# Normalised x of later batches computed by tokens and transposed by DMA, with its steps, banks and loads rearranged

## The chip, the cores and the metric

The kernel runs on one core of one Trainium2 chip. The metric is the device time of one execution in microseconds (us). A profiled execution shows a span about 2 us shorter than the device time (319.4 us for 321.2 before), so spans are compared with spans and times with times.

## The reference

Linear attention, an RMS norm per head, and a bilinear feed-forward:

```
kv  = einsum('bhsd,bhse->bhde', k, v)          # 8 batches, 8 heads, 576 tokens, head size 64
x   = einsum('bhsd,bhde->bhse', q, kv)
x   = x / sqrt(mean(x*x, over the 64) + 1e-6) * g_norm
x   = x.transpose(0, 2, 1, 3).reshape(4608, 512)
out = ((x @ w_a) * (x @ w_b)) @ w_out          # 512 -> 1536 -> 512
```

## The kernel before

x is kept transposed in SBUF (feature on the partition, token along the row), because the kernel's feed-forward takes it so as `rhs`. The profile shows a matmul as two records: a load of the one operand, its weights (`lhsT`, 128x128 in 98 ns in the feed-forward), and a pass over the columns of the other (`rhs`, 512 columns from one start to the next in 0.216 us). Results go to PSUM, used here as eight banks of 128 x 512 numbers (`P[:, 0]` to `P[:, 7]`). The kernel writes a bank anew only when its last reader is done; in the changed kernel TensorE waits for that twice, 0.58 us each. The feed-forward goes over nine strips of 512 tokens. While TensorE works on strip s, the x of batch s+1 is put between its matmuls, in "slots": slot(n) comes after unit n of the strip, slot(n - 0.5) in the middle of unit n. A unit is one block of 128 features of the hidden layer: four matmuls with w_a (part a), four with w_b (part b), all 512 columns wide. Units 12 to 15 of the count are the four output groups. With FC = 12, a strip has 12 x 8 + 4 x 12 = 144 matmuls of 512 columns.

```
def x(self, p, i0):                    # a pair of heads: 2 matmuls of 288 columns
    for h in range(2):
        nc.tensor.matmul(P[:, i0 + h, 0:HF], lhsT=kvb[self.b % 2][:, p, :],
                         rhs=self.qT[:, p, h * HF : (h + 1) * HF], start=True, stop=True)

def psq(self, p, i0):                  # square, ScalarE
    nc.scalar.activation(sq[p % 3], P[:, i0 : i0 + 2, 0:HF], AF.Square)

def pss(self, p, i0, hs=(0, 1)):       # mean over the head's 64 partitions: 2 more matmuls
    for h in hs:
        nc.tensor.matmul(P[:, i0 + h, 0:HF], lhsT=ones, rhs=sq[p % 3][:, h, :], start=True, stop=True)
    nc.scalar.activation(rs[p % 3][...], P[...], AF.Abs_reciprocal_sqrt, bias=eps_t)

def pst(self, p, x0, hs=(0, 1)):       # x * g * rs, written straight into xt
    for h in hs:
        nc.vector.scalar_tensor_tensor(out=xt[p][:, t0 : t0 + HF], in0=P[:, x0 + h, 0:HF],
                                       scalar=g_col, in1=rs[p % 3][:, h, :], ...)

# ... cut ...
def ffn_ab(s, fc, between=None):       # a unit: PSUM banks in turn out of 0, 1, 2
    i = n_ab[0]; n_ab[0] += 2
    u = Unit(s, fc, i % 3, (i + 1) % 3)
    u.part_a()                         # 4 matmuls, then ScalarE casts the bank to SBUF
    if between: between()              # slot(n - 0.5)
    u.part_b()                         # 4 matmuls, then VectorE multiplies the two

def slot(A, s, n):
    kb = P[:, 7, 0 : NP * D]...
    if s < 3: k0, xs, ss = 6, (7, 9.5, 12, 13.5), (8, 10.5, 12.5, 14)
    else:     k0, xs, ss = 2, (4, 7, 10, 12), (5, 8, 11, 13)
    if n == k0: ...  # kv of the batch: 40 small matmuls
    if n in xs: ...  # x, psq
    if n in ss: ...  # pss, pst
```

The q of batches 2 to 7 is cast to bf16 in DRAM by GpSimd's DMAs (`load_late`, with k and v of the batch) and transposed from there by a DMA that SyncE issues (`transpose_q`). In `load_late`, a tiny GpSimd copy reads the transposed q of the batch before, and so holds the loads back until that transpose has landed (the first one waits 15.02 us for it, until 62.92, and the loads follow from 63.76). SyncE also issues the stores, and in the trace its issues follow the order of the program: strip 0's stores from 46.54 us, the q transpose behind them from 53.37.

## Time and profile before

| | before |
|---|---|
| device time, median | 321.61 us (3 runs, 321.01 to 321.7) |
| span of the profiled run | 319.4 us |
| TensorE busy | 312.0 us, 98% |
| VectorE, ScalarE, GpSimd busy | 39%, 39%, 22% |

The page's table of engines (PE is TensorE's matmuls, PEld its weight loads, DVE VectorE, ACT ScalarE, POOL GpSimd; SP, further down, is SyncE):

```profile
PE 312.0 (98%) x1848; PEld 150.2 (47%) x1883; DVE 124.6 (39%) x218; ACT 125.3 (39%) x217; POOL 70.2 (22%) x94
```

Busy time alone would not prove that TensorE is the limit. The windows view of strips 1, 2 and 3 (columns: window, its length, then busy us and count of each engine, clock, DMA share, GB/s) comes nearer: 33.7 of 33.9 us.

```profile
50.37:84.27 33.90, 33.69 (x199) 16.30 (x201) 14.33 (x25) 14.79 (x25) 6.57 (x7) 1.00 1.11 151
84.27:118.16 33.89, 33.68 (x197) 16.25 (x200) 13.35 (x22) 14.29 (x24) 12.56 (x14) 1.00 1.07 122
118.16:152.06 33.90, 33.74 (x198) 16.28 (x200) 13.45 (x22) 14.39 (x24) 7.17 (x8) 1.00 1.27 151
```

The chain of waits in strip 5 shows what the strip is made of (columns: start, length, what; L255 and L309 are the feed-forward, L158 is kv, L235 is x, L209 the mean):

```profile
191.30 0.75 PE P L158 x40
...
195.61 0.24 PE P L235 x2
195.86 1.73 PE P L255 x8
197.59 0.25 PE P L209 x2
...
214.84 5.18 PE P L309 x24
220.02 3.24 PE P L255 x15
```

24 matmuls of 512 columns take 5.18 us, 0.216 each; 144 of them take 31.1. Strip 7, which has no next batch to compute, bears this out: it takes 31.08 us (253.75 to 284.83). Four pairs for x and four for the mean, at 0.24 to 0.25 us, take about 1.95. kv takes 0.75, and about 0.1 more passes before it. TensorE's timeline shows this in strip 1 (start, length, and so on; from start to start a part of four matmuls takes 0.86 us, the lengths given are longer and overlap; the `x3` is a part with one record missing):

```profile
61.59 1.03 PE L255 MATMUL P<-xt,wb_t 128*128 128x512 bf16 x4
62.55 0.82 PE L158 MATMUL P<-vtl,ktl 128*64 128x64 bf16 x40
63.30 1.04 PE L255 MATMUL P<-xt,wa_t 128*128 128x512 bf16 x3
```

The sum is the strip, 33.9 us. So TensorE waits for no other engine in the middle strips, and work taken off it shortens them; a better order of the same matmuls promises little there.

### The profile page before, as it was taken

The numbers are of one execution on the slowest core, as the hardware profiler recorded it, in microseconds if no ns is written. First come the engines' busy times: TensorE is split into PE (matmuls) and PEld (weight loads), VectorE is DVE, ScalarE is ACT, GpSimd is POOL, SyncE is SP. The second block draws the span as 40 slices with busy tenths as digits, with TensorE's granted clock in tenths as the row PEclk, the third lists the DMA queues.
The fourth block names the chain that finished last, engine by engine and source line by source line (L and its number), as shares of the span: only waits on it lengthen the run. The fifth ranks groups of instructions, "written<-read, shape, count | busy, mean of one in ns | idle before, by whom it ended". The sixth has DMA issues, their size and how long they took to land.

```text
span 319.4 us, 4695 instructions
## 1 busy us (share of the span) xinstructions
PE 312.0 (98%) x1848; PEld 150.2 (47%) x1883; DVE 124.6 (39%) x218; ACT 125.3 (39%) x217; POOL 70.2 (22%) x94
## 2 busy tenths in 40 slices
PE   8899999999999999999999999999999999999995
PEld 3444454444445444444444444444544444444443
DVE  5543344444244333452245324532364243313421
ACT  3733165354335443542445225542454323123310
POOL 8944990070043080350070000000000000000000
PEclk9999999999999999999999999999999999999999
DMA  8999999999379999899499150003000200020002
GB/s 182 197 196 199 201 182 230 141 95 161 99 92 159 135 123 211 81 138 173 119 94 129 66 139 2 0 35 100 0 2 14 90 30 0 34 84 18 0 33 99
DMA packets 79308, 32.60 MB, mean 102 GB/s; under 512 B 49974, under 2 KB 74806, under 8 KB 79286
## 3 DMA queue, kind: packets, MB, share of 16 engines
q0 software_dynamic: 59120, 18.44, 53.0%
q1 hardware_dynamic: 19810, 13.44, 17.1%
q10 hardware_dynamic: 356, 0.43, 0.4%
q8 instruction: 14, 0.23, 0.3%
q14 instruction: 8, 0.07, 0.1%
HBM read 37.75 MB, written 12.98 MB: 159 GB/s over the span
## 4 chain that ended last, share of the span: by engine, by line
PE 93%; POOL 3%; DMA 2%; issue 1%; ACT 0%; POOLq 0%
PE P L255 58%; PE P L309 29%; PE P L209 2%; PE P L235 2%; DMA wb_t<-in_moe_w_b_dram 2%; PE P L158 2%; POOL vt L106 1%; POOL qt L106 1%; POOL kt L106 1%; PE P L182 0%; POOL wa_t L367 0%; POOL wb_t L367 0%; ACT o_end L540 0%; POOL ident masks.py:199 0%; POOL ident masks.py:197 0%
## 5 line engine op out<-in xcount | busy, mean ns | idle before, releaser
L273 DVE TENSOR_TENSOR ab<-P,asb 128x512 bf16<-128x512 f32 x108 | 74.5, 691 | 124.0 <-PE P L255 120.7
L255 PE MATMUL P<-xt,wa_t 128*128 128x512 bf16 x422 | 111.2, 379 | 0.9 <-issue 0.2
L255 PE MATMUL P<-xt,wb_t 128*128 128x512 bf16 x421 | 110.1, 379 | 0.3
L309 PE MATMUL P<-wo_t,ab 128*128 128x512 bf16 (+1 forms) x431 | 97.5, 373 | 0.7
L269 ACT CAST asb<-P 128x512 bf16<-128x512 f32 x108 | 63.0, 585 | 85.3 <-PE P L255 83.8
L255 PEld LDWEIGHTS <-wb_t 128*128 128x128 bf16 x432 | 42.3, 98 | 50.6 <-DMA wb_t<-in_moe_w_b_dram 0.5
L309 PEld LDWEIGHTS <-ab 128*128 128x128 bf16 x444 | 43.1, 98 | 45.4
L255 PEld LDWEIGHTS <-wa_t 128*128 128x128 bf16 x432 | 41.7, 98 | 45.1 <-issue 0.5
L223 DVE SCALAR_TENSOR_TENSOR xt<-P,g_col,rs 128x288 bf16<-128x288 f32 x64 | 30.1, 513 | 29.6 <-ACT rs L213 29.6
L205 ACT ACTIVATE sq<-P 128x576 bf16<-128x576 f32 x31 | 20.2, 650 | 25.1 <-PE P L235 23.2
L213 ACT ACTIVATE rs<-P,eps_t 128x576 f32<-128x576 f32 (+1 forms) x33 | 23.9, 727 | 14.9 <-PE P L209 14.6
L322 ACT COPY osb<-P 128x512 f32<-128x512 f32 x17 | 10.0, 586 | 46.0 <-PE P L309 43.6
L324 DVE COPY osb<-P 128x512 f32<-128x512 f32 x18 | 12.4, 691 | 26.9 <-PE P L309 26.8
L129 POOL DMA_DIRECT2D qs<-in_q_dram x12 | 19.6, 1636 | 2.2 <-issue 2.1
L126 POOL COPY gate<-qT 1x1 bf16<-1x1 bf16 x5 | 0.9, 176 | 83.2 <-DMA qT<-qs 83.2
L209 PE MATMUL P<-sq,ones 128*128 128x288 bf16 x64 | 13.2, 286 | 0.5 <-ACT sq L205 0.4
L235 PE MATMUL P<-qT,kvb 128*128 128x288 bf16 x56 | 11.4, 286 | 0.0
L169 ACT CAST kvb<-P 64x256 bf16<-64x256 f32 (+1 forms) x20 | 6.0, 301 | 11.1 <-PE P L158 11.0
L209 PEld LDWEIGHTS <-ones 128*128 128x128 bf16 x64 | 6.2, 98 | 7.5 <-issue 0.4
L235 PEld LDWEIGHTS <-kvb 128*128 128x128 bf16 x56 | 5.5, 98 | 6.0
L121 POOL DMA_DIRECT2D wo_t<-in_moe_w_out_dram x12 | 6.4, 530 | 6.7 <-DMA wb_t<-in_moe_w_b_dram 3.3
L337 PE MATMUL P<-zeros 128*128 128x512 bf16 x16 | 6.2, 532 | 1.2 <-DVE eps_t L352 1.2
(55 smaller groups left out, 82.6 us busy)
## 6 DMA issues: line engine op xcount, KB each, us to landing
out_dram<-osb SPq DMA_DIRECT2D x23, 256.0 KB, 2.0
qs<-in_q_dram POOLq DMA_DIRECT2D x12, 288.0 KB, 6.6
ktl<-in_k_dram POOLq DMA_DIRECT2D x6, 512.0 KB, 8.7
vtl<-in_v_dram POOLq DMA_DIRECT2D x6, 512.0 KB, 10.7
out_dram<-osb SPq DMA_DIRECT2D x13, 128.0 KB, 2.4
wo_t<-in_moe_w_out_dram POOLq DMA_DIRECT2D x12, 128.0 KB, 6.0
wa_t<-in_moe_w_a_dram POOLq DMA_DIRECT2D x5, 256.0 KB, 9.2
wb_t<-in_moe_w_b_dram POOLq DMA_DIRECT2D x5, 256.0 KB, 9.8
```

Of the source, the lines that this page charges most:

```text
L129: nc.gpsimd.dma_start(out=d[:, hs, :], in_=q[b, hs].rearrange("h t d -> t h d"))
L205: nc.scalar.activation(sq[p % 3], P[:, i0 : i0 + 2, 0:HF], AF.Square)
L209: nc.tensor.matmul(P[:, i0 + h, 0:HF], lhsT=ones, rhs=sq[p % 3][:, h, :], start=True, stop=True)
L213: nc.scalar.activation(rs[p % 3][:, h0:h1, :], P[:, i0 + h0 : i0 + h1, 0:HF], AF.Abs_reciprocal_sqrt, bias=eps_t,)
L223: nc.vector.scalar_tensor_tensor(out=xt[p][:, t0 : t0 + HF], in0=P[:, x0 + h, 0:HF], scalar=g_col, in1=rs[p % 3][:, h, :], op0=ALU.mult, o ...
L235: nc.tensor.matmul(P[:, i0 + h, 0:HF], lhsT=kvb[self.b % 2][:, p, :], rhs=self.qT[:, p, h * HF : (h + 1) * HF], start=True, stop=True,)
L255: nc.tensor.matmul(self.a if w is wa_t else self.b, lhsT=w[:, kc, self.fc * 128 : (self.fc + 1) * 128], rhs=xt[kc][:, t0 : t0 + STRIP], st ...
L269: nc.scalar.copy(self.t, self.a)
L273: nc.vector.tensor_mul(abt[self.s % 2][self.fc], self.b, self.t)
L309: nc.tensor.matmul(P[:, i, e0:e1], lhsT=abt[s % 2][fc][:, g * 128 : (g + 1) * 128], rhs=wo_t[:, fc, e0:e1], start=(fc == 0), stop=(fc == F ...
L322: nc.scalar.copy(t, P[:, i, :])
L324: nc.vector.tensor_copy(t, P[:, i, :])
```

## The change

The intent: for batches 2 to 7, compute x with tokens on the partitions instead. Then the mean over a head's 64 numbers runs along the row, and VectorE does it; the eight matmuls with `ones` go. The price is that x comes out the wrong way round for the feed-forward, so a transposing DMA puts it into `xt`. The 576 tokens of a batch are five chunks, 4 of 128 tokens and one of 64, each in one bank. Four matmuls of 128 columns make a chunk, with q as the weights.

```diff
+        def tx(self, c, i):                       # slot x
+            t0 = c * 128
+            n = min(128, S - t0)                  # 64 for the last chunk
+            for p in range(NP):
+                nc.tensor.matmul(P[0:n, i, p * 128 : (p + 1) * 128],
+                    lhsT=self.qT[:, p, t0 : t0 + n], rhs=kvb[self.b % 2][:, p, :], start=True, stop=True)
+            nc.scalar.activation(sqt[c % 3][0:n], P[0:n, i, :]..., AF.Square)
+        def tss(self, c):                         # slot x + 0.5
+            nc.vector.reduce_sum(sst[c % 3][0:n], sqt[c % 3][0:n], axis=mybir.AxisListType.X)
+        def trs(self, c):                         # slot x + 1
+            nc.scalar.activation(rst[c % 3][0:n], sst[c % 3][0:n], AF.Abs_reciprocal_sqrt, ...)
+            nc.gpsimd.tensor_mul(sqt[c % 3][0:n], rst[c % 3][0:n]..., g_all[0:n]...)
+        def txt(self, c, i):                      # slot x + 2.5
+            nc.vector.tensor_mul(t[0:n], P[0:n, i, :]..., sqt[c % 3][0:n])
+            nc.sync.dma_start_transpose(xt[:, :, t0 : t0 + n], t[0:n]...)
 ...
+    AB = (4, 1, 2, 0)                             # banks of the units, in turn; were 0, 1, 2
 ...
+    nc.sync.dma_start(out=g_all, in_=g_norm.partition_broadcast(128))
+    transpose_q(2)
     ffn_o(0, 0, X[0])                             # strip 0's output groups and stores
 ...
-    transpose_q(2)
 ...
-        if s < 3:
-            k0, xs, ss = 6, (7, 9.5, 12, 13.5), (8, 10.5, 12.5, 14)
-        else:
-            k0, xs, ss = 2, (4, 7, 10, 12), (5, 8, 11, 13)
+        k0, xs = (5, (6.5, 7.5, 8.5, 9.5, 10.5)) if s == 1 else (2, (3.5, 5, 6, 7.5, 8.5))
 ...
+        for c, x in enumerate(xs):
+            i = 5 + c % 3                         # the chunk's bank
+            if n == x:         A.tx(c, i)
+            elif n == x + 0.5: A.tss(c)
+            elif n == x + 1:   A.trs(c)
+            elif n == x + 2.5: A.txt(c, i)
 ...
+            if s == 1 and n == 3:
+                load_late(3)
+            if b + 1 < B and n == (12 if s == 1 else 8):
+                transpose_q(b + 1)
+            if b + 2 < B and n == 13:
+                load_late(b + 2)
```

(Cut: buffers, the counting of the banks, and the old lines of the loads and transposes. The four `xt` tiles become one; the buffers of the start-up are used again for x by tokens.)

More of the change, by code (lines that the diff above doesn't have):

```diff
@@ L70 @@
     kvb = [sb([128, NP, 128], BF16, f"kvb{i}") for i in range(2)]
-    xt = [sb([128, n_tok], BF16, f"xt{i}") for i in range(KC)]
+    xt = sb([128, KC, n_tok], BF16, "xt")
     abt = [[sb([128, STRIP], BF16, f"ab{i}_{f}") for f in range(FC)] for i in range(2)]
@@ L75 @@
     rs = [sb([128, 2, HF], FP32, f"rs{i}") for i in range(3)]
+    k_x = sb([128, 2 * EC * D], FP32, "k_x")
+    k32 = k_x[0:EP].rearrange("p (h c d) -> p h c d", h=2, c=EC)
+    sqt = [sb([128, H, D], FP32, f"sqt{i}") for i in range(2)]
+    sqt.append(k_x[:, 0 : H * D].rearrange("p (h d) -> p h d", h=H))
+    sst = [sb([128, H], FP32, f"sst{i}") for i in range(3)]
+    rst = [sb([128, H], FP32, f"rst{i}") for i in range(3)]
+    g_all = sb([128, D], FP32, "g_all")
     o_sb = [sb([128, d_model], FP32, f"osb{i}") for i in range(4)]
@@ L83 @@
     warm = sb([128, 1], FP32, "warm")
-    k32 = sb([EP, 2, EC, D], FP32, "k32")
-    v32 = sb([EP, 2, EC, D], FP32, "v32")
-    q32 = sb([EP, 2, EC, D], FP32, "q32")
+    qv = [sb([128, 2 * EC * D], FP32, f"qv{i}") for i in range(2)]
+    q32, v32 = (t[0:EP].rearrange("p (h c d) -> p h c d", h=2, c=EC) for t in qv)
+    x_tok = [t.bitcast(BF16).rearrange("p (c h d) -> p c h d", c=3, h=H) for t in qv]
     qc = sb([EP, EC, 2 * D], BF16, "qc")
@@ L223, in pst @@
                 nc.vector.scalar_tensor_tensor(
-                    out=xt[p][:, t0 : t0 + HF],
+                    out=xt[:, p, t0 : t0 + HF],
                     in0=P[:, x0 + h, 0:HF],
@@ L241, in x @@
                 )
+        def tx(self, c, i):
+            t0 = c * 128
+            n = min(128, S - t0)
+            for p in range(NP):
+                nc.tensor.matmul(
+                    P[0:n, i, p * 128 : (p + 1) * 128],
+                    lhsT=self.qT[:, p, t0 : t0 + n],
+                    rhs=kvb[self.b % 2][:, p, :],
+                    start=True,
+                    stop=True,
+                )
+            nc.scalar.activation(
+                sqt[c % 3][0:n], P[0:n, i, :].rearrange("t (h d) -> t h d", h=H), AF.Square
+            )
+        def tss(self, c):
+            n = min(128, S - c * 128)
+            nc.vector.reduce_sum(sst[c % 3][0:n], sqt[c % 3][0:n], axis=mybir.AxisListType.X)
+        def trs(self, c):
+            n = min(128, S - c * 128)
+            nc.scalar.activation(
+                rst[c % 3][0:n],
+                sst[c % 3][0:n],
+                AF.Abs_reciprocal_sqrt,
+                bias=eps_t[0:n],
+                scale=1.0 / D,
+            )
+            nc.gpsimd.tensor_mul(
+                sqt[c % 3][0:n],
+                rst[c % 3][0:n].unsqueeze(2).to_broadcast([n, H, D]),
+                g_all[0:n].unsqueeze(1).to_broadcast([n, H, D]),
+            )
+        def txt(self, c, i):
+            t0 = c * 128
+            n = min(128, S - t0)
+            t = x_tok[c // 3][:, c % 3]
+            nc.vector.tensor_mul(
+                t[0:n], P[0:n, i, :].rearrange("t (h d) -> t h d", h=H), sqt[c % 3][0:n]
+            )
+            t0 += self.b * S
+            nc.sync.dma_start_transpose(
+                xt[:, :, t0 : t0 + n], t[0:n].rearrange("t h d -> t (h d)")
+            )
     class Unit:
@@ L257, in mm @@
                     lhsT=w[:, kc, self.fc * 128 : (self.fc + 1) * 128],
-                    rhs=xt[kc][:, t0 : t0 + STRIP],
+                    rhs=xt[:, kc, t0 : t0 + STRIP],
                     start=(kc == KORD[0]),
@@ L277, in rest, with ab_bank @@
             self.part_b(kcs)
+    AB = (4, 1, 2, 0)
     n_ab = [0]
+    def ab_bank():
+        n_ab[0] += 1
+        return AB[(n_ab[0] - 1) % len(AB)]
     def ffn_ab(s, fc, between=None):
-        i = n_ab[0]
-        n_ab[0] += 2
-        u = Unit(s, fc, i % 3, (i + 1) % 3)
+        u = Unit(s, fc, ab_bank(), ab_bank())
         u.part_a()
@@ L449 @@
     u3.part_b()
-    n_ab[0] = 1
+    n_ab[0] = 0
     for fc in range(4, FC):
@@ L482 @@
     u1.rest((3,))
-    n_ab[0] = 0
+    n_ab[0] = 1
     def slot(A, s, n):
         kb = P[:, 7, 0 : NP * D].rearrange("q (p e) -> q p e", e=D)
-        if s < 3:
-            k0, xs, ss = 6, (7, 9.5, 12, 13.5), (8, 10.5, 12.5, 14)
-        else:
-            k0, xs, ss = 2, (4, 7, 10, 12), (5, 8, 11, 13)
+        k0, xs = (5, (6.5, 7.5, 8.5, 9.5, 10.5)) if s == 1 else (2, (3.5, 5, 6, 7.5, 8.5))
         if n == k0:
@@ L496, in slot @@
             A.kv_out(slice(0, NP), kb)
-        if n in xs:
-            p = xs.index(n)
-            A.x(p, X[0])
-            A.psq(p, X[0])
-        if n in ss:
-            p = ss.index(n)
-            A.pss(p, SS)
-            A.pst(p, X[0])
+        for c, x in enumerate(xs):
+            i = 5 + c % 3
+            if n == x:
+                A.tx(c, i)
+            elif n == x + 0.5:
+                A.tss(c)
+            elif n == x + 1:
+                A.trs(c)
+            elif n == x + 2.5:
+                A.txt(c, i)
     for s in range(1, N_STRIP - 1):
@@ L511 @@
             if n >= FC:
-                i = O if n % 2 == 0 else n_ab[0] % 3
-                n_ab[0] += n % 2
-                ffn_o(s, n - FC, i, amid)
+                ffn_o(s, n - FC, ab_bank() if n % 2 else O, amid)
             elif s > 1 or n > 1:
@@ L518 @@
                 slot(A, s, n)
-            if n == 8 and b + 1 < B:
-                if s > 1:
-                    transpose_q(b + 1)
-                    if b + 2 < B:
-                        load_late(b + 2)
-                else:
-                    load_late(3)
-        if s == 1:
-            transpose_q(3)
-            load_late(4)
+            if s == 1 and n == 3:
[4 more added lines that the diff above has]
+                load_late(b + 2)
     last = N_STRIP - 1
```

## The prediction

> **What bounds the kernel.** TensorE. The busy table gives PE 312.0 of 319.4 us (98%), clock 1.0. The chain of waits is 93% PE, and after about 16 us it is an unbroken run of matmuls. From the timeline, a middle strip takes 33.89 us (191.30 to 225.20): 144 feed-forward matmuls of 512 columns at about 0.2155 us each make 31.03, the x and mean-square matmuls of the next batch (16 of 288 columns, a pair in 0.24 us) 1.95, the kv matmuls about 0.9. The sum is the strip, so there is no stall to win back; only removed columns count. VectorE and ScalarE are 39% busy.
>
> **What the change does, for batches 2 to 7.** The 8 x matmuls and 8 ones matmuls (4608 columns) become 20 x matmuls of 128 columns (2560). In the start-up of this trace six matmuls of 128 columns with fresh 128-column weights span 0.49 us, of which the last one's 0.218 is latency: 54 ns apart. [...] 20 x 0.056 = 1.12 us against 1.95: 0.83 us saved per batch, 5.0 us over six batches, all on the critical path.
>
> **Added work, off the path.** Per batch: five squares on ScalarE (about 0.6 us each, as the 128x512 cast, 0.585) and five tiny roots instead of 650+741 ns x4; on VectorE five reductions[...] and five 128x512 products (0.69) instead of 8x513 ns; five two-input products on GpSimd[...]. Five transposing DMAs land far before use. In strips 2 to 6 every consumer has at least a unit (1.73 us) of slack.
>
> **Where it gives some back: strip 1.** Steps are one unit apart. Chunk 3 reuses the bank of chunk 0, whose last VectorE product is queued after unit 9's product; TensorE asks for the bank one half-unit (0.86 us) later. Before, VectorE starts 0.28 us after the matmul stream's end and takes 0.69; then 0.69 for the chunk's product: free at about 1.65 us. So TensorE stalls 0.8 us at chunk 3 and again at chunk 4: 1.6 us. Also kv moves ahead by one unit, to about 60.7 us, while v of batch 2 lands at about 61.3 (issue 46.3 and 47.2, 14.1 to landing): estimate 0.6 us of stall. The q transpose ahead of strip 0's stores starts near 50 instead of 53.4 us; the stores wait, but four output buffers hold the strip, so nothing stalls. The fourth unit bank and the late g load save nothing: no wait of TensorE there before.
>
> **Sum.** 321.6 - 5.0 + 1.6 + 0.6 = 318.8 us. Range 316.4 to 321.2. Faster by over 2%: 0.03; within 2%: 0.93; slower by over 2%: 0.04.
>
> **What would show it.** Strips 2 to 6 about 33.05 us each; strip 1 about 35; the new x matmuls about 0.22 us per chunk; two waits of PE on the VectorE product of chunks 0 and 1 in strip 1, 0.8 us each; a wait of kv on v's DMA below 1.5 us; [...]PE wait on the transposing DMA at strip starts: none.
>
> **What would make it wrong.** [...] (b) GpSimd products much slower, or held up behind late q/k/v loads on the same queue: the chunk product then blocks VectorE and with it the units. (c) The transposed q of batch 2 or k/v landing later through contention with stores: strip 1 stalls by microseconds. (d) No stall in strip 1 at all: 316.6.

The sum came to 318.8 us. But the 56 ns of its "20 x 0.056" had nothing behind it in the trace before, which gives 54; e5 below measures 56. At 54 ns the saving would be 1.95 - 1.08 = 0.87 us per batch, 5.2 in all, and the sum 318.6 us.

## The result and the profile after

| | before | after |
|---|---|---|
| device time, median | 321.47 us (4 runs: the three above and one more) | 319.15 us (4 runs, 319.05 to 319.26) |
| span | 319.4 us | 317.4 us |
| strip 1 | 33.90 us | 34.65 us |
| each of strips 2 to 6 | 33.9 us | 33.28 us |

The ratio of the times is 0.993, 95% interval 0.9913 to 0.9947: within 2% of before, and clearly a little faster. Ratios here are the mean time of one kernel's fast runs over the mean of the other's in the same rounds, so not quite the ratio of the medians. The result is correct.

The page's table, and the same three strips:

```profile
PE 310.9 (98%) x1907; PEld 147.6 (46%) x1907; DVE 138.2 (44%) x230; ACT 115.8 (37%) x229; POOL 101.8 (32%) x124
```
```profile
50.60:85.25 34.65, 33.48 (x206) 15.85 (x204) 16.60 (x27) 13.22 (x27) 11.76 (x12) 1.00 1.26 168
85.25:118.53 33.28, 33.28 (x205) 15.76 (x204) 15.71 (x24) 12.75 (x26) 18.49 (x19) 1.00 1.22 145
118.53:151.81 33.28, 33.28 (x205) 15.79 (x204) 15.70 (x24) 12.75 (x26) 11.86 (x12) 1.00 0.88 122
```

In strips 2 and 3 TensorE is busy for the whole of the window by this count, so here too it waits for no other engine; the strip is 0.62 us shorter because it has fewer columns. (The ends of matmuls are modelled in this profile, so busy does not mean streaming all the time: gaps of 0.1 us, as below, don't show in this count. Strip 7 is 31.08 us here too, so what changed lies in the next batch's work.) Strip 1 alone is longer than before, and there TensorE is not busy for 1.17 us.

Where it waits is in TensorE's timeline of strip 1 (in brackets: the idle time before, and what ended it):

```profile
66.36 0.39 PE L258 MATMUL P<-kvb,qT 128*128 128x128 bf16 x4
66.58 1.03 PE L312 MATMUL P<-xt,wb_t 128*128 128x512 bf16 x4
...
69.40 1.03 PE L312 MATMUL P<-xt,wa_t 128*128 128x512 bf16 x4
71.01 0.38 PE L258 MATMUL P<-kvb,qT 128*128 128x128 bf16 x4 [0.58 <-DVE qv L292]
...
72.09 1.03 PE L312 MATMUL P<-xt,wa_t 128*128 128x512 bf16 x4
73.70 0.38 PE L258 MATMUL P<-kvb,qT 128*64 128x128 bf16 x4 [0.58 <-DVE qv L292]
74.02 1.04 PE L312 MATMUL P<-xt,wb_t 128*128 128x512 bf16 x4
```

A full chunk (66.36 to 66.58) takes 0.22 us. Chunks 3 and 4 start only when VectorE has released a bank (L292 is `txt`). And VectorE's timeline shows why that comes late:

```profile
69.67 0.69 DVE L330 TENSOR_TENSOR ab<-P,asb 128x512 bf16<-128x512 f32 x1 [0.67 <-PE P L312]
70.28 0.68 DVE L292 TENSOR_TENSOR qv<-P,sqt 128x512 bf16<-128x512 f32 x1
```

The product of chunk 0 stands behind the product of unit 9 (L330), which itself waits for TensorE. It frees the bank at 70.96. TensorE's part a of unit 10 begins at 69.40 and takes 0.86, so it asks for the bank at 70.26.

One more place is worth a look, the last chunk of a strip (this is strip 3):

```profile
135.82 1.03 PE L312 MATMUL P<-xt,wa_t 128*128 128x512 bf16 x4
136.78 0.41 PE L258 MATMUL P<-kvb,qT 128*64 128x128 bf16 x4
137.12 1.04 PE L312 MATMUL P<-xt,wb_t 128*128 128x512 bf16 x4
138.00 0.38 PE L312 MATMUL P<-xt,wa_t 128*128 128x512 bf16 x1
```

The form `128*64` says weights of 64 columns (64 tokens). Part a streams until 136.68 (135.82 + 0.86), and the next part starts at 137.12: the last chunk, with half the tokens, takes 0.44 us where a full one takes 0.22. Nothing is shown as waiting on another engine.

### The profile page after: what moved, and what is told of

It is laid out like the page before. It is cut to its first block, busy times and chain, and to the rows that moved or that the text cites. A ratio compares the mean times of both kernels' runs of the same rounds, so it can differ in the third digit from the quotient of the medians.

```text
span 317.4 us, 4979 instructions
## 1 busy us (share of the span) xinstructions
PE 310.9 (98%) x1907; PEld 147.6 (46%) x1907; DVE 138.2 (44%) x230; ACT 115.8 (37%) x229; POOL 101.8 (32%) x124
## 4 chain that ended last, share of the span: by engine, by line
PE 85%; DMA 7%; POOL 4%; issue 1%; DVE 1%; ACT 0%; POOLq 0%; DVEq 0%
PE P L312 52%; PE P L369 28%; DMA wb_t<-in_moe_w_b_dram 6%; PE P L258 2%; PE P L168 2%; DMA vt<-in_v_dram 2%; POOL qt L116 1%; POOL wo_t L131 1%; POOL kt L116 1%; POOL vt L116 1%; POOL wa_t L427 0%; POOL wb_t L427 0%; DVE qv L292 0%; PE P L192 0%; PE P L219 0%
## 5 line engine op out<-in xcount | busy, mean ns | idle before, releaser
L330 DVE TENSOR_TENSOR ab<-P,asb 128x512 bf16<-128x512 f32 x108 | 74.5, 691 | 111.3 <-PE P L312 93.8
L369 PE MATMUL P<-wo_t,ab 128*128 128x512 bf16 (+1 forms) x444 | 95.6, 373 | 0.0
L282 POOL TENSOR_TENSOR sqt<-rst,g_all 128x512 f32<-128x512 f32 (+1 forms) x24 | 25.0, 1044 | 97.4 <-ACT rst L275 97.4
L271 DVE TENSOR_REDUCE sst<-sqt 128x8 f32<-128x512 f32 (+1 forms) x24 | 16.2, 676 | 0.8 <-ACT sqt L265 0.8
L292 DVE TENSOR_TENSOR qv<-P,sqt 128x512 bf16<-128x512 f32 (+1 forms) x24 | 16.2, 678 | 0.0
L265 ACT ACTIVATE sqt<-P 128x512 f32<-128x512 f32 (+1 forms) x24 | 14.2, 593 | 1.6 <-PE P L258 1.6
L258 PEld LDWEIGHTS <-qT 128*128 128x128 bf16 (+1 forms) x120 | 8.9, 100 | 9.5 <-issue 4.0
L258 PE MATMUL P<-kvb,qT 128*128 128x128 bf16 (+1 forms) x120 | 11.7, 220 | 1.2 <-DVE qv L292 1.2
L275 ACT ACTIVATE rst<-sst,eps_t 128x8 f32<-128x8 f32 (+1 forms) x30 | 9.0, 301 | 4.3 <-DVE sst L271 4.3
L233 DVE SCALAR_TENSOR_TENSOR xt<-P,g_col,rs 128x288 bf16<-128x288 f32 x16 | 7.5, 512 | 5.2 <-ACT rs L223 5.2
L282 POOL TENSOR_TENSOR k_x<-rst,g_all 128x512 f32<-128x512 f32 x6 | 6.3, 1044 | 7.0 <-ACT rst L275 7.0
## 6 DMA issues: line engine op xcount, KB each, us to landing
vtl<-in_v_dram POOLq DMA_DIRECT2D x6, 512.0 KB, 12.5
```

The source lines that it names most:

```text
L258: nc.tensor.matmul(P[0:n, i, p * 128 : (p + 1) * 128], lhsT=self.qT[:, p, t0 : t0 + n], rhs=kvb[self.b % 2][:, p, :], start=True, stop=True,)
L265: nc.scalar.activation(sqt[c % 3][0:n], P[0:n, i, :].rearrange("t (h d) -> t h d", h=H), AF.Square)
L271: nc.vector.reduce_sum(sst[c % 3][0:n], sqt[c % 3][0:n], axis=mybir.AxisListType.X)
L282: nc.gpsimd.tensor_mul(sqt[c % 3][0:n], rst[c % 3][0:n].unsqueeze(2).to_broadcast([n, H, D]), g_all[0:n].unsqueeze(1).to_broadcast([n, H, D]),
L292: nc.vector.tensor_mul(t[0:n], P[0:n, i, :].rearrange("t (h d) -> t h d", h=H), sqt[c % 3][0:n])
L330: nc.vector.tensor_mul(abt[self.s % 2][self.fc], self.b, self.t)
```

## Experiments

Two questions were open. Is strip 1 longer because of the bank, or because of late data? And why are strips 2 to 6 at 33.28 us and not at the predicted 33.05? Seven kernels were run; all gave the correct result.

### e1_spread: strip 1's steps farther apart

```diff
-        k0, xs = (5, (6.5, 7.5, 8.5, 9.5, 10.5)) if s == 1 else ...
+        k0, xs = (5, (6.5, 8, 9, 10.5, 11.5)) if s == 1 else ...
```

> The changed kernel with the x steps of strip 1 at 6.5, 8, 9, 10.5, 11.5 instead of one unit apart; nothing else. Theory (bank reuse: in strip 1 the matmuls of chunks 3 and 4 wait for the bank that chunks 0 and 1 leave half a unit too late): both waits of TensorE on the VectorE product are gone, strip 1 goes from 34.65 to about 33.3 us, the time falls by about 1.35 us to 317.8, ratio to before about 0.989. Rival (strip 1 is longer because its q, k and v arrive late or because the loads hold up GpSimd): the wait stays or moves, time within 0.3 us of 319.15.

Measured: 317.67 us, ratio to before 0.9881 (0.9866 to 0.9897). Strip 1 took 33.28 us, as strips 2 to 6, and no wait of TensorE on VectorE's chunk product is left in the profile. The theory's numbers hold. Chunks 3 and 4 in TensorE's timeline, without a bracket:

```profile
70.99 1.03 PE L312 MATMUL P<-xt,wa_t 128*128 128x512 bf16 x4
71.85 0.39 PE L258 MATMUL P<-kvb,qT 128*128 128x128 bf16 x4
...
72.94 1.46 PE L369 MATMUL P<-wo_t,ab 128*128 128x512 bf16 x6
74.33 0.41 PE L258 MATMUL P<-kvb,qT 128*64 128x128 bf16 x4
```

kv and chunk 0 kept their steps, so late q, k or v would still have shown. A late GpSimd product could have been hidden by the later chunks; against it stands that VectorE's product of chunk 0 followed at once on unit 9's in the changed kernel (70.28, no wait for GpSimd), and e6, where the steps stay.

### e6_banks: the same steps, other banks

The units get three banks as before the change, the chunks four.

```diff
-    AB = (4, 1, 2, 0)
+    AB = (1, 2, 0)
-    n_ab[0] = 1                # at the start of strip 1's ring
+    n_ab[0] = 2
-            i = 5 + c % 3
+            i = 4 + c % 4
```

> The changed kernel with the banks dealt otherwise: units over three banks as before the change, chunks of x over four (4 to 7) instead of three; the steps stay. Theory (the wait in strip 1 is for a bank, and the fourth bank of the units is not needed): chunk 3 finds a free bank and chunk 4 takes the one chunk 0 left a unit and a half earlier, so both waits go, the units don't wait, time about 317.8, ratio 0.989. Rival (VectorE is behind in strip 1, with product, chunk product and reduction in one step): units then wait for their banks instead and the time stays near 319.

Measured: 317.76 us, ratio 0.9876 (0.9857 to 0.9895); strip 1 and strips 2 to 6 all 33.28 us. Chunks 3 and 4 start without a wait:

```profile
69.42 1.03 PE L312 MATMUL P<-xt,wa_t 128*128 128x512 bf16 x4
70.28 0.39 PE L258 MATMUL P<-kvb,qT 128*128 128x128 bf16 x4
...
71.36 1.03 PE L312 MATMUL P<-xt,wa_t 128*128 128x512 bf16 x4
72.32 0.41 PE L258 MATMUL P<-kvb,qT 128*64 128x128 bf16 x4
```

So the wait was for the bank, not for time on VectorE, and the fourth bank, which the change gave to the units, was not needed by them.

### e2_tail128: the last chunk with 128 columns of weights

```diff
         def tx(self, c, i):
-            t0 = c * 128
-            n = min(128, S - t0)
+            n = 128
+            t0 = min(c * 128, S - n)     # tokens 448 to 575: the first 64 are computed twice
 ...
             nc.sync.dma_start_transpose(
-                xt[:, :, t0 : t0 + n], t[0:n]...
+                xt[:, :, t0 : t0 + m], t[n - m : n]...     # m = 64: only the new ones go out
```

> The changed kernel, but chunk 4 of each batch takes tokens 448 to 575 as weights (128 columns instead of 64) and transposes only its last 64 rows out. Theory (the 64-column weights of the last chunk cost about 0.1 us of switch and 0.34 us of run where a full chunk costs 0.225): each of the strips 1 to 6 is 0.21 us shorter, strips 2 to 6 at 33.07 us, the time falls by about 1.3 us to 317.9, ratio about 0.989. Rival (the strips miss their predicted 33.05 us because 128-column matmuls come slower than 56 ns apart in general, or because chunk 4 waits for its bank): strips stay at 33.28 us, time within 0.3 us of 319.15.

Measured: 317.79 us, ratio 0.9884 (0.9869 to 0.9899). Strips 2 to 6 take 33.05 or 33.06 us. TensorE's timeline of the same place in strip 3, where the last chunk now begins at once and takes 0.23 us:

```profile
135.34 1.03 PE L313 MATMUL P<-xt,wa_t 128*128 128x512 bf16 x4
136.20 0.39 PE L258 MATMUL P<-kvb,qT 128*128 128x128 bf16 x4
136.43 1.03 PE L313 MATMUL P<-xt,wb_t 128*128 128x512 bf16 x4
```

Twice the work in this chunk is faster by 0.21 us. Banks and steps are those of the changed kernel, so chunk 4's late start was no wait for its bank. And the strip's sum closes: 31.08 for the feed-forward, 0.85 for kv and 1.12 for 20 matmuls make 33.05. Strip 1 took 34.54 us here, 1.49 more than the others: this is what its two waits cost when nothing hides behind them. (In the changed kernel the difference is 1.37, since the last chunk's late start there falls into the wait.)

### e5_double_x: the price of one small matmul

```diff
-            for p in range(NP):
+            for p in [p for p in range(NP) for _ in range(2)]:
                 nc.tensor.matmul(P[0:n, i, p * 128 : (p + 1) * 128], ...)
```

> The changed kernel with every x matmul of batches 2 to 7 issued twice into the same place (same result). It measures the price of one such matmul with its weight load in the running kernel. Theory (TensorE is the limit and a 128-column matmul takes 54 to 56 ns, one with 64-column weights about 80): 24 chunks cost 4 x 0.055 = 0.22 us more each and 6 tail chunks about 0.33, 7.3 us in all, time about 326.5. [...] Rival (they fit into slack): no change.

Measured: 325.86 us, ratio 1.013 (1.0112 to 1.0149), 6.7 us more than the changed kernel. Strips 2 to 6 take 34.39 or 34.40 us, 1.12 more: 20 matmuls, 56 ns each. That rules out that they fit into slack. In the changed kernel's profile each of the 120 matmuls has its own weight load (L258, 120 of them, 0.1 us each). It also corrects my own detail: I expected the last chunk's matmuls to be dearer (0.33 us for four more, an estimate from the 0.34 us of four in the changed kernel), and they are not. TensorE's timeline of strip 2 shows the last chunk with eight matmuls (columns as above):

```profile
104.49 1.03 PE L312 MATMUL P<-xt,wa_t 128*128 128x512 bf16 x4
105.44 0.63 PE L258 MATMUL P<-kvb,qT 128*64 128x128 bf16 x8
106.01 1.04 PE L312 MATMUL P<-xt,wb_t 128*128 128x512 bf16 x4
```

From start to start it is 0.57 us; with four it was 0.34 (136.78 to 137.12). Four more cost 0.23. So the narrow weights don't slow each matmul here: they cost a fixed sum, about 0.1 us before them (136.68 to 136.78) and as much after (0.34 - 0.23), for going from 128-column weights to 64 and back.

The weight loads in the trace of the changed kernel show where this time goes. Between wide weights TensorE's load runs ahead: the one for the part a of 135.82 starts at 135.61, 0.21 us before it. The load of the first narrow weights starts only at 136.78, together with its matmul and after the stream before has ended, and so does the next wide one, at 137.12. kv's first narrow load in strip 2 (90.53, together with its matmul) is late in the same way. In e6 the view of waits has six gaps of up to 0.4 us before the loads of x, as many as there are last chunks; in e3, where the last chunks are wide and no bank is waited for, it lists none. Why loads don't run ahead at a change of width is not shown.

### e4_q_after_stores: the q transpose back behind the stores

```diff
-    transpose_q(2)
     ffn_o(0, 0, X[0])
 ...
+    transpose_q(2)
     u0 = Unit(1, 0, 2, 3)
```

> The changed kernel with the q transpose of batch 2 put back behind strip 0's stores. Theory (the transpose is off the path, but GpSimd's loads for batch 3 wait for it and GpSimd's first product comes after them, with only 0.4 us to spare): q lands about 1 us later, 62.5 instead of 61.6 us, x of chunk 0 at 64.4 us still does not wait, GpSimd's first product comes about 1 us later and the first wait in strip 1 grows by about 0.5 us: time 319.2 to 319.9. Rival (the move ahead is what makes the change work): strip 1 longer by 2 us or more, time above 321.

Measured: 320.44 us (6 runs, 319.89 to 321.11), ratio 0.9964 (0.9947 to 0.9981), by the medians 1.3 us slower than the changed kernel, and outside what I expected. The rival's number (above 321) is not reached by the median, but it is by the profiled run, 321.06, one of the two slowest of the six: its strip 1 took 36.63 us, 1.98 more. The sizes below are that run's; in most of the others the loss must be smaller. Two waits make it. From TensorE's and VectorE's timelines:

```profile
61.06 0.32 PE L168 MATMUL P<-vtl,ktl 128*64 128x64 bf16 x8
62.33 0.69 PE L168 MATMUL P<-vtl,ktl 128*64 128x64 bf16 x32 [0.96 <-DMA vtl<-in_v_dram]
...
72.93 0.38 PE L258 MATMUL P<-kvb,qT 128*128 128x128 bf16 x4 [1.37 <-DVE qv L292]
```
```profile
72.19 0.69 DVE L292 TENSOR_TENSOR qv<-P,sqt 128x512 bf16<-128x512 f32 x1 [0.69 <-POOL sqt L282]
```

The second is the one I expected: GpSimd's loads wait for the transposed q, which came at 63.8 instead of 61.6 us, its first product starts only after them, at 71.06 instead of 68.80, and VectorE's chunk product waits for it (TensorE's wait grows from 0.58 to 1.37). The first I had forgotten: with the stores ahead (SyncE issues them from 47.11 us here; in the changed kernel from 58.07, behind the transpose at 50.38), v of batch 2 takes 14.5 to 14.9 us from issue to landing, against 12.5 to 12.8 in the changed kernel, and kv now stands one unit earlier than it did before. So the move of the transpose earns nothing itself, but the earlier steps of strip 1 need it.

### e7_old_x_new_order: only the order of transposes and loads

The kernel before, x in its old form and at its old steps, with `transpose_q` and `load_late` where the change has them (the last lines of the diff above, and the two moved lines of `transpose_q(2)`).

> The kernel before, with only the order of transposes and loads of the changed one: q of batch 2 ahead of strip 0's stores, loads of batch 3 at step 3, later ones at step 13, transposes at step 12 or 8. x stays in the old form. Theory (these moves carry no gain by themselves): within 0.3 us of before. Rival (part of the 2.3 us comes from them): 1 us or more faster.

Measured: 321.23 us, ratio 0.9986 (0.9971 to 1.0). All its strips take 33.89 or 33.90 us. By itself the order gives nothing that the runs can tell from zero. The v of batch 2 lands 10.2 to 10.5 us after issue here, in the kernel before 14.0 to 14.3: the order does bring it in earlier, but the old steps don't use that.

### e3_both: e1 and e2 together

> Both edits together, the spread steps of strip 1 and the full last chunk. If both theories hold and are independent, the gains add: about 2.6 us, time 316.5, ratio about 0.985, strips 1 to 6 all 33.07 us. If the rivals hold, 319.

Measured: 316.34 us (4 runs, 315.89 to 316.47), ratio 0.9836 (0.982 to 0.9852). All of strips 1 to 6 take 33.05 or 33.06 us: the two gains add. This version beats both kernels, by 5.1 us and 2.8 us of the medians. In its chain of waits VectorE, which had 1% in the changed kernel, no longer appears. (DMA's share, 7% there and 2% here, is loads before strip 1, which the two edits don't touch.)

```profile
PE 94%; POOL 3%; DMA 2%; issue 0%; ACT 0%; POOLq 0%
```

## Why the prediction was right, point by point

The time was predicted as 318.8 us and is 319.15. But it came out so near because mis-sized terms partly cancelled: the saving was put 1.3 us too high, the losses in strip 1 0.8 too high. That part is luck. In the sum "321.6 - 5.0 + 1.6 + 0.6":

| term | predicted | profile | shown by |
|---|---|---|---|
| fewer columns, six strips | -5.0 | -3.7 (6 x 0.62) | strips 2 to 6; e2 |
| two waits for a bank in strip 1 | +1.6 | +1.37 | e1, e6 |
| kv waits for v | +0.6 | 0 | timeline of strip 1; e4, e7 |
| start-up and end | 0 | +0.3 (0.23 before strip 1, 0.1 after strip 7) | strips' starts only |
| sum | -2.8 | -2.0 | spans 319.4 and 317.4 |

The device times differ by 2.3 us (medians), the two spans by 2.0; one profiled run of each is not exact to 0.3.

- **TensorE is the limit: right. "Only removed columns count": not quite.** e5 adds 120 matmuls that change nothing, and all of them appear in the time. But e2 adds columns of weights and streams as many as before, and is faster by 0.22 or 0.23 us a strip: the change of width counts too.
- **"54 ns apart": right, but the step "20 x 0.056 = 1.12 us against 1.95: 0.83 us saved per batch" left out a cost.** The 128-column matmuls do come 56 ns apart (e5). What was missing is the fixed 0.21 us for the last chunk's 64-column weights. So a batch saved 0.62 us and not 0.83. The full saving of 0.84 us appears in e2, where the strip is 33.05 us as predicted. The hint was there before: kv, with 64-column weights, begins at 62.55 us in strip 1 of the kernel before, 0.1 after its predecessor's stream must have ended (61.59 + 0.86).
- **The waits in strip 1: right in place, number and cause.** They came at chunks 3 and 4, on the products of chunks 0 and 1. The size was 0.75 each rather than 0.8 (e2: 1.49 for both): I put 0.69 us between the starts of two VectorE products in a row, and the trace has 0.61.
- **kv's wait for v: wrong.** I took v's landing at 61.3 us from the trace of before, where the stores were ahead of the transpose. The change itself reverses that, and v landed by 60.2 us (issue 47.4, at most 12.8 to landing), before kv at 61.06. e4 restores the old order, and the wait is there, 0.96 us.
- **"The fourth unit bank and the late g load save nothing": right for the bank (e6).** The g load was not tried by itself.
- **"The q transpose ahead ... nothing stalls": right, but too weak.** Without it the new steps of strip 1 lose 1.3 us by the medians, 1.98 in the profiled run (e4).
- **GpSimd's product: 1.04 us**, VectorE's reduction 0.68 us. Neither is in the way in strips 2 to 6.
- **"Five transposing DMAs land far before use": right, though no time was given.** The 30 of them landed 2.3 to 7.2 us after issue, with a median of 2.8, and TensorE waits for none. The q transposes, one per batch, have a median of 5.2; that of batch 2 took 11.1. What makes the difference was not tested.
- **Left open:** the 0.23 us by which strip 1 begins later (50.60 against 50.37). The chain of the changed kernel has ahead of it a wait on batch 1's v (5.33 us, to 39.76); the seven other kernels begin strip 1 anywhere from 50.41 to 50.62, so I take it for the scatter of the start-up's loads. No run tests it.

## What to carry to other kernels

When one engine is busy without a gap, count what is taken off it, and price it from a place in the trace with the same shape in every dimension, the weights' width too: a narrower remainder can cost more than a full tile that computes some of it twice (0.44 against 0.23 us here). When consumers are moved closer together, work out for each reused buffer when its last reader is issued, not only how long it runs: here VectorE's product of chunk 0 (70.28) stood behind that of unit 9 (69.67), which itself had waited 0.67 us for TensorE, the very engine that asks for the buffer. And do not carry a landing time of a DMA over from the old trace when the change reorders the DMAs around it (v of batch 2: 14.0 to 14.3 us before, 12.5 to 12.8 after).
